# Seven products of half blocks in the second layer of an attention and feed-forward kernel

## The chip, the cores and the metric

The kernel runs on one core of a Trainium2 chip. A core has a matrix engine (PE, with its weight loads listed apart as PEld), a vector engine (DVE), a scalar engine (ACT), a general engine (POOL) and a queue engine (SP) that issues most DMAs. The metric is the device time of one execution in microseconds; of several runs the median is taken. Lower is better.

## The reference

Eight batches of 8 heads, 512 tokens, 32 states, head width 64. Tokens attend to states and states to tokens; the two results, 544 rows a batch, go through a two-layer network of width 512, 2048, 512 with a gate between the layers. All in float32.

```python
scores = scale * np.matmul(x, state.transpose(0, 1, 3, 2))
a = softmax(scores); xread = np.matmul(a, state)            # 512 token rows a batch
a2 = softmax(scale * np.matmul(state, x.transpose(...)))
sread = np.matmul(a2, x)                                    # 32 state rows a batch
x = np.concatenate([xread, sread], axis=2)...               # (8 * 544, 512)
h = x @ w_in
g = h * np.clip(h + 3.0, 0.0, 6.0) / 6.0
return g @ w_out
```

## The kernel before

**Joint weights.** `xread @ w_in` is `a @ (state @ w_in)`. So the kernel makes, for each batch, the joint weights `wp` (heads times states, 256 rows, by 2048 columns) and multiplies the attention weights `aT` by them; `xread` is never formed. The 2048 columns of the first layer lie in 16 blocks of 128. A **step** is one batch and one block: `first(n)` makes the first layer of the step in a PSUM bank `ps_h` (512 tokens wide), ACT and DVE make the gate `g` from it, `split` makes the pair `g_hi`, `g_lo`, and two steps later (`LAG = 2`) `second(n)` adds the block's share of the second layer to four banks `acc`, one for each 128 tokens. Steps 0 to 127 are the token rows of batches 0 to 7; steps 128 to 143 are the 256 state rows of all batches.

**Pairs.** A product of two float32 operands is made by `product` (line 1166) as three matmuls of 16-bit pairs, high by high, high by low, low by high (float32 rounded in batches 0 and 1, float16 from batch 2, `HALF_FROM = 2`). A step of the token rows has 6 matmuls in the first layer and 12 in the second, each 512 columns wide, each with a weight load of its own.

**Where the joint weights come from.** For batches 1 to 3 `wprime` makes them batch by batch on PE from float32 operands (line 631: 64 rows by 32 columns, eight tiles of the array side by side). For batches 4 to 7 `joined` (line 698) makes them for four batches at once, in eight calls between steps 33 and 72, from float16 pairs of `w_in` (`w_in_terms`); the results go out to DRAM, and `wprime_loaded` brings them back in each batch.

**The state rows.** Their first layer is made ahead of step 128 by `states_first`: seven products of half blocks (instead of eight) for each half of the columns, on sums of `w_in` that `w_in_terms` made and stored, with sums, gate, transposes and 32 small DMAs behind them. Steps 128 to 143 then only split and multiply by the second layer (`states_halves`).

**What sets the order.** `Plan.order` is a list scheduler: each operation has an engine (T is PE, V DVE, S ACT, P POOL, Q the SP queue), a cost, a rank (when it is due, in steps) and the keys it reads and writes; it places the ready operation of lowest rank and hands out buffers. Lists such as `PLANS`, `FETCH` and `CONVERTED` give ranks to the attention of the next batch and to conversions. Each engine then executes its list in order.

Of the kernel before, what the change touches and what calls it, by code (L numbers as in the profile page):

```python
# [46 lines left out]
CONVERTED = [23, 23, 21, 23, 25, 25, 30, 26, 36, 40, 38, 41, 35, 44, 43, 46]  # L47
EXTRA_FROM = 130
GROWN = {3: "ot", 4: "xb", 5: "raw", 6: "raw", 7: "ot"}
PLANS = [[0, 4, 10, 4, 5, 3, 12, 7], [-2, 5, -1, 16, 5, 4, 3, 7], [0, 1, 3, 8, 5, 3, 4, 8], [-3, -1, 6, 7, 5, 5, 6, 9], [-3, 3, 5, 4, 6, 2, 4, 7], [4, 6, -10, 11, 9, 10, -6, 11], [-2, 3, -2, 5, 4, 5, 15, 6]]  # L50
FETCH = [[4, 4], [19, 19], [25, 25], [43, 37], [57, 57], [64, 80], [93, 82]]
STATES_AT = 15
MAXIMA_AT = 22
WEIGHTS_AT = 17
OPENING_ROWS = 708
SQUEEZE = 0.5
PLAIN = 1
STATES = [108, 107, 116, 1.75, 1.5]
EARLY = 5
BY_TWO = (0, 0)  # L60
TERMS = [76, 4, 7.5]
JOINED = 4
JOINED_AT = [33, 38, 53, 57, 57, 64, 62, 72]
STATES_JOINED = 18
AHEAD = 5
FORCED = []
LOADED = [-5, 12.5]
STAGED = [('wp', 'wp'), ('ot', 'aT'), ('aT', 'ot'), ('ot', 'wp'), ('wp', 'wp'), ('aT', 'wp'), ('aT', 'wp'), ('wp', 'ot')]
PREP = [9, -27]
SUMS = 70  # L70
CURVE = 2
BY_SCALAR = ()

# [207 lines left out]
def tile_state_attention_then_hardswish_ffn(  # L281
# [65 lines left out]
            "raw": 3, "ot": 2, "xb": 1, "st_raw": 1, "stT": 2, "tmp": 8, "top": 2, "aT": 2, "m1": 3, "s1": 3, "nm2": 3, "r2": 2, "wp": 2, "g": 2,  # L347
# [41 lines left out]

    def get(key, make):  # L390

        if key[:2] not in made:
            made[key[:2]] = make()
        return made[key[:2]]
# [31 lines left out]

    plain = lambda b, i: b == 0 and i < PLAIN
# [197 lines left out]
    def all_heads(b, out, moving, by_pairs=False):  # L625

        for q in range(NQ):
            for u in range(NG):
                rows, cols = slice(u * D, (u + 1) * D), slice(q * NS, (q + 1) * NS)
                at = (q + 2 * u) % NQ if by_pairs else q  # L630
                nc.tensor.matmul(  # L631
                    out[q // 2 if by_pairs else u][at * NS : (at + 1) * NS, :],
                    made["stT", b][rows, cols], moving(q)[rows],
                    start=True, stop=True,
                )
# [14 lines left out]
    def states_joined(rank, after):  # L650

        n_b = B - JOINED
        raw_key, key = (("tmp", ("joined", k)) for k in ("raw", "all"))
        raw = lambda: tmp(raw_key).rearrange("p (b e) -> p b e", b=n_b)
        of_q = lambda t: t.rearrange("p (q n b) -> p b q n", q=NQ, b=n_b)
        for b in range(n_b):
            for u in range(NG):
                for k in range(D // NS):
                    rows = slice((u * D // NS + k) * NS, (u * D // NS + k + 1) * NS)
                    Q(rank, 25.0, lambda b=b, u=u, k=k, rows=rows: nc.sync.dma_start(  # L660
                        raw()[rows, b].rearrange("n (q c) -> n q c", c=NS),
                        st_v[JOINED + b, :, :, u, k * NS : (k + 1) * NS].rearrange("q n c -> n q c")),
                      (), [(*raw_key, b, u, k)], after, cost=0.65)
            V(0.22, rank, lambda b=b: nc.vector.transpose(
                of_q(tmp(key))[:, b], raw()[:, b].rearrange("p (q n) -> p q n", n=NS)),
                [(*raw_key, b, u, k) for u in range(NG) for k in range(D // NS)], [(*key, b)])
        plan.told += [None] * 6

    def states_paired(rank):
        key = ("tmp", ("joined", "all"))  # L670
        split(rank, lambda: states_16(0), lambda: states_16(1), lambda: tmp(key),
              [(*key, b) for b in range(B - JOINED)], [(*states_key, h) for h in range(2)], 0.62, "delta", X)

    states_key = ("tmp", ("joined", "16"))

    def states_16(h):
        return half_bits(tmp(states_key), 2 * S)[:, h * S : (h + 1) * S]

    def joined(p, m, s0):
# [40 lines left out]
        if s0 in FORCED:  # L720
            plan.ops[first_of[s0 - 2]][4].add(run_at)
# [750 lines left out]
    def w_in_terms(p, m, rank, after):  # L1472
# [17 lines left out]
        if m not in own:  # L1490
            after = [*after, *items]
# [348 lines left out]
```

## Time and profile before

| | |
|---|---|
| median of 3 runs | 616.17 us (614.4 to 618.34) |
| the profiled execution | 613.97 us, of it the span 612.2 us |
| PE busy | 605.7 us, 99% |
| DVE busy | 472.2 us, 77% |
| ACT busy | 334.8 us, 55% |
| POOL busy | 3.2 us, 1% |

PE's granted clock is at its upper level, 2.4 GHz, in every slice of the page after the first. A busy PE is one with a matmul in flight; the time from the start of one to the start of the next is what a matmul costs in a row of them, and it is shorter than the duration that is listed for one.

### The profile page before, as it was taken

Reading aid. Unit: us, or ns where it says so; the run is one execution under the profiler, and the core shown is the slowest. Engines: PE = TensorE matmul, PEld = TensorE weight load, DVE = VectorE, ACT = ScalarE, POOL = GpSimd, SP = SyncE. Lnnn points to the kernel's source line nnn. Section 1 sums busy time; section 2 is a strip of 40 time slices with the busy share of each in tenths; the row PEclk is TensorE's granted clock in tenths of the full one; section 3 lists DMA queues with packets and bytes.
Section 4 is the critical chain, followed back from the end, with each engine's and each line's share of the span. In section 5 each row is a group of like instructions: output and inputs, shape, how many; then the busy total and the mean of one; then the engine's idle time right before and its main releaser. Section 6 shows DMA issues by size and latency. Waiting matters only on the chain.

```text
span 612.2 us, 9806 instructions
## 1 busy us (share of the span) xinstructions
PE 605.7 (99%) x3650; PEld 320.7 (52%) x3650; DVE 472.2 (77%) x835; ACT 334.8 (55%) x560; POOL 3.2 (1%) x12
## 2 busy tenths in 40 slices
PE   9999999999999999999999999999999999999996
PEld 7677778777744444444444444444444444444443
DVE  6998999899989999886668746697879775355532
ACT  5888986346665556665465445444555454334332
POOL 2000000000000000000000000000000000000000
PEclk9999999999999999999999999999999999999999
DMA  8999122733673162327766262911740725551041
GB/s 290 371 235 272 52 70 35 126 113 54 96 194 54 37 172 101 146 84 176 176 232 198 53 154 54 224 38 31 178 172 15 220 87 180 187 177 31 7 131 34
DMA packets 154062, 80.45 MB, mean 131 GB/s; under 512 B 127648, under 2 KB 136224, under 8 KB 153888
## 3 DMA queue, kind: packets, MB, share of 16 engines
q1 hardware_dynamic: 153872, 79.77, 47.6%
q8 instruction: 28, 0.46, 0.3%
q14 instruction: 18, 0.15, 0.1%
q10 hardware_dynamic: 144, 0.07, 0.0%
HBM read 49.40 MB, written 24.64 MB: 121 GB/s over the span
## 4 chain that ended last, share of the span: by engine, by line
PE 90%; DMA 4%; DVE 4%; issue 1%; ACT 0%; SPq 0%; DVEq 0%
PE acc L1166 54%; PE ps_h L1166 25%; PE ps_s L1166 3%; DMA raw<-in_x_dram 2%; DMA early<-in_moe_w_out_dram 2%; PE ps_s L631 2%; PE ps_h L1123 1%; PE ps_s L698 1%; PE ps_h L698 1%; PE ps_h L631 1%; DVE w_in L502 1%; PE ps_h L1809 1%; PE acc L823 0%; DVE wp_lo L422 0%; DVE room L1354 0%
## 5 line engine op out<-in xcount | busy, mean ns | idle before, releaser
L1166 PE MATMUL acc<-w,g_hi 128*128 128x512 f16 x832 | 247.6, 379 | 0.0
L1166 PE MATMUL acc<-w,g_lo 128*128 128x512 f16 x416 | 157.7, 379 | 0.0
L1224 ACT ACTIVATE g<-ps_h,three,room 128x512 f32<-128x512 f32 x96 | 74.5, 776 | 112.7 <-PE ps_h L1166 108.2
L1227 DVE SCALAR_TENSOR_TENSOR g<-g,ps_h 128x512 f32<-128x512 f32 x128 | 87.0, 681 | 60.5 <-ACT g L1224 59.3
L1166 PEld LDWEIGHTS <-g_hi 128*128 128x128 f16 x832 | 80.0, 98 | 100.5 <-issue 6.1
L416 ACT ACTIVATE g_hi<-g 128x512 f16<-128x512 f32 x96 | 60.2, 628 | 56.3 <-DVE g L1227 45.9
L417 DVE SCALAR_TENSOR_TENSOR g_lo<-g,g_hi 128x512 f16<-128x512 f32 x96 | 65.9, 687 | 23.1 <-ACT g_hi L416 21.3
L1166 PE MATMUL ps_h<-aT_hi,wp_hi 128*128 128x512 f16 (+1 forms) x182 | 70.7, 389 | 0.5 <-DVE g L1227 0.5
L1166 PE MATMUL ps_h<-aT_lo,wp_hi 128*128 128x512 f16 (+1 forms) x182 | 69.6, 382 | 0.0
L1166 PE MATMUL ps_h<-aT_hi,wp_lo 128*128 128x512 f16 (+1 forms) x182 | 69.5, 382 | 0.0
L1166 PEld LDWEIGHTS <-g_lo 128*128 128x128 f16 x416 | 40.7, 98 | 49.1
L1166 PE MATMUL acc<-w_out_hi,g_hi 128*128 128x512 f32 x124 | 49.6, 400 | 0.0
L1166 PE MATMUL ps_h<-aT_hi,wp 128*128 128x512 f16 (+1 forms) x144 | 48.9, 380 | 0.0
L1166 PE MATMUL acc<-w_out_hi,g_lo 128*128 128x512 f32 x124 | 48.4, 390 | 0.0
L1166 PE MATMUL acc<-w_out_lo,g_hi 128*128 128x512 f32 x124 | 48.3, 389 | 0.0
L1166 PEld LDWEIGHTS <-wp_hi 128*128 128x128 f16 x256 | 25.1, 98 | 30.2
L1224 ACT ACTIVATE g<-ps_h,three 128x512 f32<-128x512 f32 x32 | 21.8, 686 | 17.2 <-PE ps_h L1166 15.8
L1166 PEld LDWEIGHTS <-wp 128*128 128x128 f16 x192 | 18.5, 98 | 22.8 <-issue 0.5
L1166 PEld LDWEIGHTS acc<-w_out_hi,g_hi 128*128 128x128 f32 x124 | 23.3, 188 | 9.3 <-issue 3.7
L1166 PE MATMUL ps_h<-aT_lo,wp 128*128 128x512 f16 (+1 forms) x72 | 27.4, 380 | 0.0
L1166 PEld LDWEIGHTS acc<-w_out_hi,g_lo 128*128 128x128 f32 x124 | 23.3, 188 | 5.0
L1166 PEld LDWEIGHTS acc<-w_out_lo,g_hi 128*128 128x128 f32 x124 | 23.3, 188 | 4.6
(222 smaller groups left out, 747.2 us busy)
## 6 DMA issues: line engine op xcount, KB each, us to landing
xb<-in_x_dram SPq DMA_DIRECT2D x32, 256.0 KB, 4.3
out_dram<-ot SPq DMA_DIRECT2D x8, 1024.0 KB, 4.8
raw<-in_x_dram SPq DMA_DIRECT2D x112, 64.0 KB, 2.7
far<-half SPq DMA_DIRECT2D x14, 512.0 KB, 3.4
terms<-far SPq DMA_DIRECT2D x14, 512.0 KB, 3.8
early<-in_moe_w_in_dram SPq DMA_DIRECT2D x5, 1023.0 KB, 6.9
raw<-raw SPq DMA_DIRECT2D x112, 32.0 KB, 2.0
raw<-in_moe_w_out_dram SPq DMA_DIRECT2D x7, 511.8 KB, 8.9
```

Source lines behind the costliest of these rows:

```text
L416: S(cost, rank, lambda: nc.scalar.mul(hi(), src(), by()), [*reads, *keys], [writes[0]], after)
L417: V_(cost, rank, lambda: nc.vector.scalar_tensor_tensor(lo(), src(), by(), hi() if hi().dtype == F16 else hi().bitcast(F32), op0=ALU.mult, ...
L502: nc.vector.scalar_tensor_tensor(d, low, 13, top_of(i).bitcast(U32), op0=ALU.logical_shift_right, op1=ALU.bitwise_or)
L631: nc.tensor.matmul(out[q // 2 if by_pairs else u][at * NS : (at + 1) * NS, :], made["stT", b][rows, cols], moving(q)[rows], start=True, st ...
L698: nc.tensor.matmul(bank(ps[i, u]), st(l)[rows, i], r()[rows, i], start=n == 0, stop=n == 2)
L1123: nc.tensor.matmul(bank(pr)[cols, u * D : (u + 1) * D], e2T(b, u)[:, j * P + q * NS : j * P + (q + 1) * NS], x_tile(b)[:, NG * q + u, j, : ...
L1166: nc.tensor.matmul(ps, l, r, start=start and k == 0, stop=stop and k == n - 1)
L1224: S_(cost + 0.05, rank, lambda: nc.scalar.activation(g(), bank(ps)[:, :width], AF.Relu, bias=three, scale=scales["1/h"]() if scaled else 1.0),
L1227: V(cost, rank, lambda: nc.vector.scalar_tensor_tensor(g(), g(), 6.0, bank(ps)[:, :width], op0=ALU.min, op1=ALU.mult), [ps], [g_key])
L1809: plan.issue(tc, lambda: nc.tensor.matmul(awake[:, :256], wake[:, :P], wake, start=True, stop=True), first_of["begun"])
```

## The change

Four edits, and ranks, buffers and lists changed with them.

- In batches 5 to 7 the second layer of the tokens is grouped: a step is now 256 tokens by two blocks (`first_grouped`, `second_grouped`), and its first layer is made of matmuls 256 columns wide. `SEVEN` names, by bits, the four groups of 256 tokens in which gates times output weights is made of seven products of half blocks instead of eight (batch 5 second group, batch 6 first, batch 7 both): the gate tile `G` holds 7 blocks of 128 columns, three of them sums made on DVE, `split` makes pairs 896 wide, the sums of the output weights `T7` are made once by `mixed_weights`, and at a group's end DVE joins the partial results.
- The input weights are converted once to float16 pairs that stay in SBUF (`w_in_paired`).
- The joint weights of batches 3 to 7 are made batch by batch on PE from float16 pairs (`wprime`, 24 matmuls for a chunk of 512 columns). `joined`, the stored joint weights and their DMAs are gone.
- The first layer of the state rows is made in steps 128 to 143 by plain products 256 columns wide (`first_states`). `states_first`, its sums, its transposes and its DMAs are gone.

```diff
 HALF_FROM = 2
+SEVEN = [0, 0, 0, 0, 0, 2, 1, 3]
+PAIRED = 3
+WPRIME_AT = [-3, -2, -2, -3]
+PAIRED_AT = [41, 32, 45, 46]
+MIXED_AT = [71, 45, 61, 59, 49, 56, 94, 78]
...
-JOINED = 4
-JOINED_AT = [33, 38, 53, 57, 57, 64, 62, 72]
...
     def wprime(b, parts, rank, banks=None, after=()):
...
         def run():
             for c, _, _, n, fs, bs in work:
+                if b >= PAIRED:
+                    for k, (l, r) in enumerate(((0, 0), (0, 1), (1, 0))):
+                        all_heads(b, [bank(k)[:, :n] for k in bs], lambda q: w_in_16(c, r)[:, q, fs], False, st_16[b](l), k)
+                    continue
                 all_heads(b, [bank(k)[:, :n] for k in bs], lambda q: w_in_of(c)[:, q, fs], b == 0)
...
+    def first_grouped(n):
+
+        b, i, _, _ = steps[n]
+        q, p = divmod(i, HF)
...
+            for k in range(2):
+                f = (2 * p + k) % FPC
+                fs = slice(f * P, (f + 1) * P)
+                product(bank(ps).rearrange("p (t k s) -> p t k s", k=2, s=P)[:, :, k],
+                        [((wh[:, u, fs], wl[:, u, fs]), (ah[:, u, ts], al[:, u, ts])) for u in range(NG)])
...
+        S_(0.73, rank, lambda: nc.scalar.activation(g(), h(), AF.Relu, bias=three, scale=scales["1/h"]()),
+           [ps, ("scale", "1/h")], [key])
+        V(0.63, rank, lambda: nc.vector.scalar_tensor_tensor(
+            g(), g(), 6.0, h(), op0=ALU.min, op1=ALU.mult), [ps], [key])
+        forms[n] = True
+        k0, k1 = 1, 5
+        if seven(b, q):
+            k0, k1 = 0, 7
+            for cost, out, one, other, op in (
+                (0.4, (5, 7), (3, 5), (1, 3), ALU.subtract), (0.53, (0, 7, 3), (3, 6), (4, 7), ALU.add),
+            ):
...
+        split(ahead(n), lambda: operand_of(n, "hi", width), lambda: operand_of(n, "lo", width), src_, [key],
+              [("g_hi", n), ("g_lo", n)], 0.08 + 0.00105 * width, G_SCALE / 4)
...
+    def second_grouped(n):
...
+        for j, parts in (
+            (0, ((0, 2, lambda: half(w(1), 0)), (1, 6, lambda: half(w(1), 1)))),
+            (2, ((0, 1, lambda: half(w(0), 0)), (1, 3, lambda: t(0)))),
+            (3, ((0, 0, lambda: t(1)), (1, 5, lambda: t(3)))),
+            (1, ((0, 4, lambda: t(2)),)),
+        ):
+            def run(j=j, parts=parts):
+                for k, a, right in parts:
+                    product(bank(acc(j))[:, k * W : (k + 1) * W], [(a_of(a, 7 * P), right())],
+                            opens and k == 0, closes and k == parts[-1][0])
+            T(0.328 * len(parts), rank, run, keys, [acc(j)])
...
+    def mixed_weights(p, rank, after):
...
-    def states_first(p, rank, after=()):
...
+    def first_states(n):
...
+            product(bank(ps)[:, :width], [((w_in_16(c, 0)[:, q, fs], w_in_16(c, 1)[:, q, fs]), (ah[:, q], al[:, q]))
+                                          for q in range(NQ)])
...
-        if 0 < b < JOINED and n % (2 * FPC) == 0:
+        if 0 < b < B and not grouped(b) and n % (2 * FPC) == 0:
             wprime(b, [(c, 0, FPC), (c + 1, 0, FPC)], n - 2.6, None, [first_of[n - 3]])
             plan.ops[first_of[n - 2]][4].add(wp_at[b, c, 0])
-        elif JOINED <= b < B and n % FPC == 0:
-            wprime_loaded(b, c, n + LOADED[1], [first_of[n + LOADED[0]]])
+        elif grouped(b) and (i in (0, FPC) if BY_PAIRS else i < HF and i % 2 == 0):
+            c, many = i // 2, 2 if BY_PAIRS else 1
+            s = n + WPRIME_AT[c]
+            wprime(b, [(c + k, 0, FPC) for k in range(many)], s - 2.6, None, [first_of[s - 3]])
+            plan.ops[first_of[s - 2]][4].add(wp_at[b, c, 0])
```

**PE in batch 7.** Of the program before, the end of one product of the state rows' first layer (`terms`), the start of a first layer of the tokens, and the start of a second layer:

```order
L1166 MATMUL ps_s<-terms,aT_lo 128x512
L1166 LDWEIGHTS wp
L1166 MATMUL ps_h<-aT_hi,wp 128x512
L1166 LDWEIGHTS wp
L1166 MATMUL ps_h<-aT_lo,wp 128x512
...
L1166 LDWEIGHTS g_hi
L1166 MATMUL acc_5470<-w_1479,g_hi 128x512
L1166 LDWEIGHTS g_hi
L1166 MATMUL acc_5470<-w_1479,g_hi 128x512
L1166 LDWEIGHTS g_lo
L1166 MATMUL acc_5470<-w_1479,g_lo 128x512
```

Of the changed program, the end of the second layer of a step with seven products (`T` is `T7`) and the start of the next step's:

```order
L1125 MATMUL acc_6021<-T_2771,g_lo 128x256
L1125 LDWEIGHTS g_hi
L1125 MATMUL acc_6029<-T_2771,g_hi 128x256
L1125 LDWEIGHTS g_hi
L1125 MATMUL acc_6029<-T_2771,g_hi 128x256
L1125 LDWEIGHTS g_lo
L1125 MATMUL acc_6029<-T_2771,g_lo 128x256
L1125 LDWEIGHTS g_hi
L1125 MATMUL acc_6004<-w_1480,g_hi 128x256
```

A seven-product step has 12 matmuls in its first layer and 21 in its second, all 256 wide, where a step before has 6 and 12 of 512; every one keeps its own weight load, and the state rows' products no longer stand between the steps. Counted over the program, 1440 matmuls are 256 wide now (576 first layers of the tokens, 672 seven products, 192 first layers of the state rows); of those 512 wide, 384 fewer are in the tokens' second layer, 288 fewer in their first, and the 84 of `states_first` are gone.

**DVE in batch 7.** Of the program before, the gates (`g`, L1227) and second halves (`g_lo`) of two steps, among the state rows' work (L1570, L1545):

```order
L1227 SCALAR_TENSOR_TENSOR g_5759<-g_5759,ps_h_5745 128x512
L417 SCALAR_TENSOR_TENSOR g_lo_5783<-g_5759,g_hi_5770 128x512
L1227 SCALAR_TENSOR_TENSOR g_5792<-g_5792,ps_h_5776 128x512
L417 SCALAR_TENSOR_TENSOR g_lo_5800<-w_in2_5692,g_hi_5794 128x256
L1570 TENSOR_TENSOR C_5633<-ps_s_5785,C_5633 128x512
L1545 SCALAR_TENSOR_TENSOR raw_5809<-raw_5809,C_5633 128x1024
L417 SCALAR_TENSOR_TENSOR g_lo_5829<-g_5792,g_hi_5821 128x512
```

Of the changed program, two steps with seven products:

```order
L1180 SCALAR_TENSOR_TENSOR G_4142<-G_4142,ps_h_5969 128x512
L1189 TENSOR_TENSOR G_4142<-G_4142 128x256
L1189 TENSOR_TENSOR G_4142<-G_4142 128x3x128
L1180 SCALAR_TENSOR_TENSOR G_4142<-G_4142,ps_h_5988 128x512
...
L415 SCALAR_TENSOR_TENSOR g_lo_6059<-G_4142,g_hi_6040 128x896
L415 SCALAR_TENSOR_TENSOR g_lo_6076<-G_4142,g_hi_6061 128x896
```

Where a step before has two DVE operations 512 wide (gate and `g_lo`), this one has four: the gate, two with sums of blocks (256 and 384 wide), and `g_lo` 896 wide. Two steps go through together: both gates with their sums, then both `g_lo`.

## Rows read from the trace of the kernel before

**Rows 1.** The page's head: span, and busy time by engine.

```profile
span 612.2 us, 9806 instructions
PE 605.7 (99%) x3650; PEld 320.7 (52%) x3650; DVE 472.2 (77%) x835; ACT 334.8 (55%) x560; POOL 3.2 (1%) x12
```

**Rows 2.** Waits of PE: engine, line, releaser: us in total, times, longest.

```profile
PE ps_h L1809 <- PEq L1824: 0.8, 1, 0.8
PE ps_h L1166 <- DVE g L1227: 0.5, 1, 0.5
```

**Rows 3.** Chain of waits, two neighbouring pieces of one step: start us, us, what.

```profile
360.74 2.59 PE acc L1166 x12
363.33 1.29 PE ps_h L1166 x6
```

**Rows 4.** Groups of PE by form: line, operands, shapes, count | busy us, mean ns.

```profile
L1166 PEld LDWEIGHTS <-g_hi 128*128 128x128 f16 x832 | 80.0, 98 | 100.5 <-issue 6.1
...
L1166 PE MATMUL ps_s<-terms,sums 128*128 128x512 f16 x48 | 11.7, 379 | 0.0
...
L1166 PE MATMUL ps_s<-terms,aT_hi 128*128 128x512 f16 x24 | 7.1, 379 | 0.0
...
L1166 PE MATMUL ps_s<-terms,aT_lo 128*128 128x512 f16 x12 | 4.5, 379 | 0.0
```

**Rows 5.** Timeline of the opening: start us, us from first to last, instruction, count.

```profile
8.17 0.60 PE L823 MATMUL acc<-ident,xb 128*128 128x128 f32 x4
8.61 0.89 PE L898 MATMUL acc<-sread_t,w_in 128*128 128x64 f32 x7
...
12.78 0.88 PEld L1809 LDWEIGHTS <-const-bfloat16-1.0 128*128 128x128 bf16 x8
...
12.89 1.06 PE L1809 MATMUL ps_h<-const-bfloat16-1.0 128*128 128x256 bf16 x8
```

**Rows 6.** Timeline of PE around one call of the joined weights.

```profile
209.58 0.38 PE L1166 MATMUL acc<-w,g_lo 128*128 128x512 f16 x1
209.89 0.82 PE L698 MATMUL ps_s<-half,tmp 64*128 64x512 f16 x6
210.55 0.81 PE L698 MATMUL ps_h<-half,tmp 64*128 64x512 f16 x6
211.29 0.61 PE L1166 MATMUL acc<-w,g_hi 128*128 128x512 f16 x2
```

**Rows 7.** Timeline of PE around float32 joint weights of batch 3, two chunks.

```profile
257.20 0.38 PE L1166 MATMUL acc<-w,g_lo 128*128 128x512 f16 x1
257.51 1.09 PE L631 MATMUL ps_s<-w_in,stT 64*32 64x512 f32 x16
...
259.39 0.61 PE L1166 MATMUL acc<-w,g_hi 128*128 128x512 f16 x2
```

**Rows 8.** Busy time by stretch: PE, PEld, DVE, ACT, POOL, then clock, DMA.

```profile
50.00:100.00 50.00, 49.53 (x336) 37.25 (x334) 48.19 (x85) 42.13 (x87) 0.00 (x0) 1.00 0.33 97
...
400.00:450.00 50.00, 50.00 (x274) 22.57 (x276) 40.25 (x63) 24.71 (x38) 0.00 (x0) 1.00 0.41 107
...
500.00:550.00 50.00, 50.00 (x234) 22.67 (x232) 25.80 (x37) 19.95 (x29) 0.00 (x0) 1.00 0.54 179
```

**Rows 9.** Groups of DVE by form.

```profile
L1227 DVE SCALAR_TENSOR_TENSOR g<-g,ps_h 128x512 f32<-128x512 f32 x128 | 87.0, 681 | 60.5 <-ACT g L1224 59.3
L417 DVE SCALAR_TENSOR_TENSOR g_lo<-g,g_hi 128x512 f16<-128x512 f32 x96 | 65.9, 687 | 23.1 <-ACT g_hi L416 21.3
...
L417 DVE SCALAR_TENSOR_TENSOR half<-raw,room,half 128x1024 f16<-128x1024 f32 x8 | 10.2, 1278 | 1.2 <-ACT half L416 1.2
...
L417 DVE SCALAR_TENSOR_TENSOR g_lo<-w_in,g_hi 128x256 f16<-128x256 f32 x16 | 6.8, 424 | 12.6 <-ACT g_hi L416 12.6
```

**Rows 10.** Groups of ACT by form.

```profile
L1224 ACT ACTIVATE g<-ps_h,three,room 128x512 f32<-128x512 f32 x96 | 74.5, 776 | 112.7 <-PE ps_h L1166 108.2 <-DVE room L1404 1.7 <-DVE raw L1089 1.2
L416 ACT ACTIVATE g_hi<-g 128x512 f16<-128x512 f32 x96 | 60.2, 628 | 56.3 <-DVE g L1227 45.9 <-PE acc L1166 10.3
```

More of the change, by code (lines that the diff above doesn't have):

```diff
@@ L388, in raw_tile, with quarter @@
         return stage.tile(list(shape), dtype, name="raw", **by_plan("raw", key)) if t is None else t
+    def quarter(key, shape, dtype=F16):
+        pool = gp if key[0] == "wp" else att
+        return get(("place", key), lambda: pool.tile(list(shape), dtype, name=key[0], **by_plan(key[0], key)))
     def get(key, make):
@@ L632, in all_heads @@
                     out[q // 2 if by_pairs else u][at * NS : (at + 1) * NS, :],
-                    made["stT", b][rows, cols], moving(q)[rows],
-                    start=True, stop=True,
+                    (made["stT", b] if left is None else left)[rows, cols], moving(q)[rows],
+                    start=not term, stop=term in (None, 2),
                 )
@@ L648, in all_heads_apart @@
                     )
[L650 to L667, printed above, removed]
@@ new lines, in pair_key, with w_in_16, pair_reads, wp_key @@
+    def pair_key(c):
+        return (f"w_in{c - 1}", "pair") if c else ("w_in", "pair")
+    def w_in_16(c, h):
+        shape = (P, 2, NQ, CH)
+        return get(pair_key(c), lambda: region(NCH - 1, shape, F16, "pair") if c == 0 else cpool.tile(
+            list(shape), F16, name="pair", tag=f"w_in{c - 1}"))[:, h]
+    def pair_reads(c, ks=range(2)):
+        return [(*pair_key(c), k, h) for k in ks for h in range(2)]
+    def wp_key(b, c, h):
+        if b >= HALF_FROM:
+            return ("wp", (b, c))
+        return ("ot", ("wp", b, c)) if 0 < b and (NCH * b + c) % 3 == 2 else ("wp", (b, c, h))
@@ L1169, in tile_state_attention_then_hardswish_ffn, with ahead, seven, G_of @@
     first_of = {}
+    def ahead(n):
+        return n if n < URGED[0] else 0.02 * n + URGED[1]
+    def seven(b, q):
+        return SEVEN[b] >> q & 1
+    def G_of(n):
+        key = ("G", n)
+        return get(key, lambda: grown_half(key))
+    def grown_half(key):
+        place = plan.home[key[:2]]
+        if place not in G_tiles:
+            if "w_in" not in G_tiles:
+                G_tiles["w_in"] = cpool.tile([P, 2, 2 * J, P], F32, name="G", tag=f"w_in{NCH - 1}")
+            G_tiles[place] = G_tiles["w_in"][:, place]
+        return G_tiles[place]
@@ L1171, in first @@
     def first(n):
         b, i, _, _ = steps[n]
+        if grouped(b):
+            first_grouped(n)
+            return
         ps = ("ps_h", n)
@@ L1229, in first @@
         if not in_32:
-            split(n, half["hi"], half["lo"], g, [g_key], [("g_hi", n), ("g_lo", n)], cost,
+            split(ahead(n), half["hi"], half["lo"], g, [g_key], [("g_hi", n), ("g_lo", n)], cost,
                   G_SCALE if scaled else None)
@@ L1431, in w_16_of, with region_gone @@
         return w_16[c][:, k % FPC]
+    def region_gone(n):
+        c, half = REGIONS[n]
+        fs = range(c * FPC, (c + 1) * FPC)
+        assert all(f in in_16 for f in fs)
+        return [m for f in fs for m in plan.readers[w_out_key(f, half)]]
     region_free = {}
@@ L1456, in converted @@
         at_16[k] = [hi16, lo16]
-        for n, (c, half) in enumerate(REGIONS):
-            if n >= NCH - 1 and n not in grown and all(f in in_16 for f in range(c * FPC, (c + 1) * FPC)):
-                grown.add(n)
-                if GROWN.get(n):
-                    plan.grow(GROWN[n], [m for f in range(c * FPC, (c + 1) * FPC) for m in plan.readers[w_out_key(f, half)]], n)
-    at_16, grown = {}, set()
-    in_16 = set()
-    pieces, operands, items, joined_of = [], [], [], {}
-    OPERANDS = (1, 2, 5, 6, 3, 4, 7)
@@ L1628, in tile_state_attention_then_hardswish_ffn @@
+    chunks, steps, segment_of = [], [], []
+    for b in range(B + 1):
+        for i in range(NF):
+            if i % FPC == 0:
+                chunks.append((b, i // FPC))
+            n = HF if grouped(b) else NF
+            steps.append((b, i, i % n == 0, i % n == n - 1))
+            segment_of.append((b, i // n))
     first_after = {}
```

456 lines of the change are left out of this document (176 added, 280 removed), and 24 rows, old and new, of the table OPENING.

## The prediction

> **What bounds the kernel now.** First the page's head: PE is busy in 605.7 of 612.2 us, DVE in 77%, ACT in 55% [rows 1]. A busy share alone would not settle it, so second the waits: after the opening the longest list entry of PE is 0.5 us, once [rows 2]. Third the chain of waits: its long middle is PE following PE, pieces of 12 matmuls in 2.59 us and 6 in 1.29 [rows 3], so 0.216 us from start to start for one float16 matmul of 512 columns, and the step of 18 costs 3.88. Nothing else is seen between the pieces. The kernel is a queue of matmuls, and a change is worth what it does to the sum of their spacings, as long as DVE keeps up. How near DVE is to its end is the fourth view: from 50 to 100 us it is busy 48.2 of 50, and PE still 49.5; from 400 to 450 it is 40.3, from 500 to 550 25.8 [rows 8]. So this order of work bears a DVE at 96%.
>
> **The change, part by part, on PE.**
>
> Removed:
> - Matmuls of 512 columns: 384 in the second layer (the grouped steps with seven products no longer have them), 288 in the first layer of batches 5 to 7, 84 in the state rows' seven products (48 + 24 + 12 [rows 4]). 756 x 0.216 = 163.2 us [rows 3].
> - `joined`: eight calls. One call runs from the end of the last slot before it (209.58 + 0.216 = 209.80) to 211.29, 1.49 us [rows 6]; eight are 12.0 us. Six slots of pairs side by side would be 1.30, so 0.20 of it goes into turning the array from one tiling to another and back.
> - The float32 joint weights of batch 3: two calls of 257.20 + 0.216 to 259.39 = 1.97 us [rows 7], 3.9 us.
>
> Together 179.1 us.
>
> Added:
> - 1440 matmuls 256 columns wide. Half of a 512 would be 0.108, but each still has its own weight load of 0.098 us [rows 4], so the load nearly fills the slot, and half is only the lower bound. The nearest row is in the opening: 8 matmuls of 16 bits, 256 wide, each with its load; the loads run 0.88 us, seven spacings and one load, so (0.88 - 0.10) / 7 = 0.111 [rows 5]. The other is the transposes, which stream as long: four from 8.17 to 8.61, 0.110 [rows 5]. I take 0.110, between the bound and the nearest row and close to that; rounding leaves that row open to 0.112, the upper bound. 1440 x 0.110 = 158.4 us (155.5 to 161.3).
> - The joint weights of batches 3 to 7 on PE from float16 pairs. No row shows float16 in eight tiles; `joined` is the nearest (float16, pairs of tiles, load hidden) and the float32 call shows that the eight tiles run side by side. A chunk is 24 matmuls, eight at a time, three slots of 0.216, and the turn of 0.20: 0.85 us. Twelve calls have one chunk (batches 5 to 7), 10.2 us; four have two (batches 3 and 4), 1.49 each as `joined`, 6.0 us. Together 16.2 us. Were the load of 0.098 not hidden in any slot, it would be 20 chunks x 3 x 0.098 = 5.9 us more, the upper bound; at the lower, the turns of the sixteen calls cost nothing, 3.2 us less.
>
> Together 174.6 us. **PE's sum: 174.6 - 179.1 = -4.5 us**, with the bounds of the 256-wide price alone -7.4 to -1.6.
>
> The Trainium skill (TensorE: Matmul & The Clock Gate, section Back-to-back issue gap) gives N / 2.4 + 2.5 ns for a warm matmul, 109.2 ns at 256 columns; by that, as an estimate, the sum would be -5.7 us. The opening's row at 0.111 says a little more than the page, and no row here says it for float16 weights that differ.
>
> **On DVE.** A seven-product step has the gate (0.68), sums 256 and 384 wide (0.42 and, between 0.42 and 0.69, 0.56), and `g_lo` 896 wide, between 0.69 and 1.28: 1.13 [rows 9]. That is 2.79 us against 1.37 for a step before, and its PE time is 33 x 0.110 = 3.63. Added too are 32 short operations for the mixed weights with their splits (about 4.3 us for each of eight, steps 45 to 94), eight `pair` conversions at 1.28 in place of sixteen `half` ones, and the joins at the end of four groups. Gone are the state rows' sums, gates and transposes, the `w_in` sums and the joined halves; the halves of the joint weights stay 8 a batch. So the early stretch, now at 96%, gets no fuller, and the late one (80 and 52%) fills up. A batch has about 17 us of the next batch's attention on DVE (22 operations of about 0.69 [rows 9] and some 2 us of small ones) and 5.5 of halves. Batch 6: 8 x 2.79 + 8 x 1.37 + 17 + 5.5 = 56 us, against PE's 8 x 3.63 + 8 x 3.91 + 3.4 for joint weights + 2 for scores = 66. That is 85%, under what the trace bears. ACT stays well under it. So I cost DVE at nothing but new waits of 0.5 us; what hides it is the next batch's attention being spread over a whole batch. If that clumps, rival 2 applies.
>
> **On SP, DMA and the ends.** About 140 DMAs go away and nothing waited for them; no gain. The opening's first 30 steps have the same work in the same order. In the last 16 steps PE now makes first layers, 2.6 us a step, and the chain behind one (ACT, DVE, ACT, DVE, each about 0.42 [rows 9]) has two steps of room; only at the last one can it show, inside the 0.5.
>
> **Sum:** -4.5 + 0.5 = -4.0 us. Against the profiled execution, 613.97, that is 610.0; the median of the runs shown stands 2.2 us above it, so 616.17 - 4.0 = **612.2 us**.
>
> **The rivals.**
> 1. *The 256-wide matmuls cost what half a 512 does and the tiled calls hide their turns in part.* 1440 x 0.108, joint weights 1 us cheaper, no new wait: -8.4 us, 607.8. For it: at 512 columns the load is wholly hidden. Against: the row at 0.111. Chance 0.20.
> 2. *DVE becomes late in the seven-product groups.* A gate there has ACT 0.78, DVE 0.68 + 0.98, ACT about 1.0 (0.63 at 512 columns, 896 here), DVE 1.13 behind it [rows 9, 10], 4.6 us with no handoffs, of 7.3 in two steps; other DVE work that comes in between has 1.7 us of room for a pair of steps. If half of a batch's attention falls into the seven-product half, DVE there has 8 x 2.79 + 8.7 + 2.8 = 33.8 us against PE's 32: 2 us lost in each of three such halves, and as much again in handoffs, +4 to +8 on the sum of PE: about 617. For it: the order puts two gates together ahead of two `g_lo`. Against: 96% was borne. Chance 0.17.
> 3. *Slower: the weight load does not fit behind 256 columns.* The place is all 1440 matmuls. A load starts with the matmul before it and lasts 0.098 us; the slot is 0.108. The sum turns at (179.1 - 16.2) / 1440 = 0.113, just above the opening's row, and 1% is lost from 0.117. With 0.120, loads that start 0.01 late, it is +10 us: 626. For it: the opening's row already lies above half of a 512, and its operands are a constant. Against: transposes with 32-bit loads keep 0.110. Chance 0.10. The Trainium skill (same page and section) says that a stream of loads and matmuls runs at 81 ns for 128 columns where an isolated one takes 56, that is, that loads show once matmuls are short; the opening's row agrees in direction, with 3 ns instead of 25.
>
> The forecast has the other 0.53.
>
> **Range and chances.** A measurement of this kernel tells about 1%, 6 us, from no change. The low end is PE's best sum without waits, -7.4, and 2 us for the scatter of the medians: 607. The high end takes in rival 2 and the unhidden loads of the joint weights: 620. Rival 3 is left out. Faster by over 1% (below 610): rival 1 and the lower part of the forecast, 0.20 + 0.12 = 0.32. Slower by over 1%: rival 3 and the end of rival 2, 0.13. Within 1%: 0.55.
>
> **What would show it.** The spacing of 256-wide matmuls in a seven-product step: 0.110 (0.108 rival 1, 0.117 and more rival 3). A single-chunk call of the joint weights: 0.85 us from slot to slot. PE's waits for `g_hi` and `g_lo` in batches 5 to 7: under 1 us in all (rival 2: 4 or more), DVE there at 85 to 90%. No `joined` pieces and no products between steps 108 and 128. I am wrong if PE's waits add up to more than the 4 us that its sum gives back, or if the 256-wide spacing depends on the operand.

## The result and the profile after

The changed kernel takes **610.0 us** (median; 608.65 to 610.17) against 615.69 for the kernel before in the same comparison: ratio 0.9897, 95% interval 0.9861 to 0.9934. Timed again beside other kernels it took 609.71, ratio 0.9905 (0.9889 to 0.992). That is 5.7 to 6.1 us, 1.0%, and the interval excludes no change. The forecast was 612.2 us in 607 to 620. The kernel before has one run more here than in the table ahead of the prediction, so its median is 615.69 and not 616.17.

The head of the page after, to be read against [rows 1]:

```profile
span 608.4 us, 11646 instructions
PE 600.8 (99%) x4654; PEld 387.0 (64%) x4654; DVE 505.8 (83%) x925; ACT 352.5 (58%) x587; POOL 3.3 (1%) x12
```

PE issues 1004 matmuls more in less time, and the work that pays for it is on DVE: 505.8 us instead of 472.2. PE's waits after (engine, line, releaser: us in total, times, longest), against [rows 2]:

```profile
PE ps_h L1772 <- PEq L1787: 0.8, 1, 0.8
PE acc L779 <- DMA xb<-in_x_dram: 0.4, 1, 0.4
PE ps_h L1125 <- DVE wp L420: 0.4, 1, 0.4
PE ps_s L631 <- DVE w_in L502: 0.4, 1, 0.4
PE ps_h L1125 <- DVE g L1349: 0.3, 1, 0.3
```

All are of the opening or of the early float32 batches; none names the tiles of a grouped step (`G`, `g_hi` or `g_lo` from `G`, `ot`). The chain of waits in batch 5, against [rows 3]:

```profile
443.40 2.29 PE acc L1125 x21
445.69 1.31 PE ps_h L1125 x12
```

2.29 / 21 and 1.31 / 12 are both 0.109 us for a matmul of 256 columns, PE still following PE. Over all such pairs of neighbours in the trace the mean from start to start is 0.1092 us. The timeline of PE's loads and of PE for one first layer of such a step:

```profile
513.90 1.30 PEld L1125 LDWEIGHTS <-wp 128*128 128x128 f16 x12
...
514.01 1.47 PE L1125 MATMUL ps_h<-aT,wp 128*128 128x256 f16 x12
```

Twelve loads span 1.30 us, eleven spacings and one load of 0.10: 0.109 again. One call of the new joint weights, on PE's timeline, which answers to [rows 6, 7]:

```profile
499.22 0.38 PE L1125 MATMUL ps_h<-aT,wp 128*128 128x256 f16 x2
499.53 0.84 PE L631 MATMUL ps_s<-pair,st 64*32 64x512 f16 x24
500.31 0.60 PE L1125 MATMUL acc<-w,g_hi 128*128 128x512 f16 x2
```

The slot of the last 256-wide matmul ends at 499.22 + 2 x 0.109 = 499.44, so the call takes 0.87 us to 500.31. The twelve calls of one chunk all take 0.87 us, the four of two chunks 1.51. DVE by form (count, then busy us and mean ns of one), against [rows 9]:

```profile
L415 DVE SCALAR_TENSOR_TENSOR g_lo<-G,g_hi 128x896 f16<-128x896 f32 x32 | 34.7, 1086 | 4.1 <-ACT g_hi L414 3.6
...
L1180 DVE SCALAR_TENSOR_TENSOR G<-G,ps_h 128x512 f32<-128x512 f32 x48 | 32.8, 683 | 14.0 <-ACT G L1178 13.9
...
L1189 DVE TENSOR_TENSOR G<-G 128x384 f32<-128x384 f32 x32 | 17.9, 558 | 1.1
L1189 DVE TENSOR_TENSOR G<-G 128x256 f32<-128x256 f32 x32 | 13.6, 425 | 1.1
```

And busy time by stretch (stretch, its length, then PE, PEld, DVE, ACT, POOL, granted clock, DMA share, GB/s), against [rows 8]: the early stretch, and those of a group of seven in batches 5, 6 and 7.

```profile
50.00:100.00 50.00, 49.64 (x336) 37.36 (x335) 48.67 (x86) 42.17 (x86) 0.00 (x0) 1.00 0.36 108
...
420.00:451.00 31.00, 31.00 (x395) 25.11 (x393) 27.27 (x46) 17.59 (x26) 0.00 (x0) 1.00 0.23 53
451.00:482.00 31.00, 31.00 (x273) 24.32 (x271) 28.14 (x47) 18.68 (x30) 0.00 (x0) 1.00 0.09 15
514.00:545.00 31.00, 31.00 (x286) 27.79 (x285) 25.94 (x50) 17.35 (x22) 0.00 (x0) 1.00 0.00 1
```

DVE is at 88, 91 and 84% there, and PE is busy throughout.

### The profile page after: what moved, and what is told of

It is laid out like the page before. It is cut to its first block, busy times and chain, and to the rows that moved or that the text cites. A ratio compares the mean times of both kernels' runs of the same rounds, so it can differ in the third digit from the quotient of the medians.

```text
span 608.4 us, 11646 instructions
## 1 busy us (share of the span) xinstructions
PE 600.8 (99%) x4654; PEld 387.0 (64%) x4654; DVE 505.8 (83%) x925; ACT 352.5 (58%) x587; POOL 3.3 (1%) x12
## 4 chain that ended last, share of the span: by engine, by line
PE 89%; DMA 6%; DVE 2%; SPq 0%; issue 0%; ACT 0%; DVEq 0%; ACTq 0%
PE acc L1125 54%; PE ps_h L1125 29%; PE ps_s L631 4%; DMA early<-in_moe_w_in_dram 3%; DMA raw<-in_x_dram 2%; PE ps_h L1082 1%; PE ps_h L631 1%; DMA xb<-in_x_dram 1%; DVE w_in L502 1%; SPq L597 0%; DVE g_lo L420 0%; DVE aT L420 0%; DVE wp L420 0%; PE ps_s L1082 0%; SPq L617 0%
## 5 line engine op out<-in xcount | busy, mean ns | idle before, releaser
L1125 PE MATMUL acc<-w,g_hi 128*128 128x512 f16 (+1 forms) x768 | 204.7, 353 | 0.0
L1125 PE MATMUL ps_h<-aT,wp 128*128 128x256 f16 (+2 forms) x1050 | 188.1, 324 | 0.7 <-DVE wp L420 0.4
L1125 PE MATMUL acc<-w,g_lo 128*128 128x512 f16 (+1 forms) x384 | 135.3, 352 | 0.0
L1125 PEld LDWEIGHTS <-wp 128*128 128x128 f16 x864 | 84.2, 98 | 44.4 <-issue 0.8
L1178 ACT ACTIVATE G<-ps_h,three,room 128x512 f32<-128x512 f32 x48 | 37.4, 778 | 49.9 <-PE ps_h L1125 48.3
L414 ACT ACTIVATE g_hi<-G 128x896 f16<-128x896 f32 (+2 forms) x64 | 46.8, 734 | 32.9 <-DVE G L1189 19.8
L1346 ACT ACTIVATE g<-ps_h,three,room 128x512 f32<-128x512 f32 x48 | 37.2, 776 | 47.9 <-PE ps_h L1125 47.8
L415 DVE SCALAR_TENSOR_TENSOR g_lo<-G,g_hi 128x896 f16<-128x896 f32 (+2 forms) x64 | 52.2, 819 | 12.4 <-ACT g_hi L414 11.7
L1125 PE MATMUL acc<-T,g_hi 128*128 128x256 f16 x256 | 43.7, 273 | 0.0
L1125 PE MATMUL acc<-T,g_lo 128*128 128x256 f16 x128 | 34.9, 273 | 0.0
```

The source lines that it names most:

```text
L414: S(cost, rank, lambda: nc.scalar.mul(hi(), src(), by()), [*reads, *keys], [writes[0]], after)
L415: V_(cost, rank, lambda: nc.vector.scalar_tensor_tensor(lo(), src(), by(), hi() if hi().dtype == F16 else hi().bitcast(F32), op0=ALU.mult, ...
L1125: nc.tensor.matmul(ps, l, r, start=start and k == 0, stop=stop and k == n - 1)
L1178: S_(0.73, rank, lambda: nc.scalar.activation(g(), h(), AF.Relu, bias=three, scale=scales["1/h"]()), [ps, ("scale", "1/h")], [key])
L1346: S_(cost + 0.05, rank, lambda: nc.scalar.activation(g(), bank(ps)[:, :width], AF.Relu, bias=three, scale=scales["1/h"]() if scaled else 1.0),
```

## The experiments

Two questions stood after the result: which part of the change brings the 6 us, and which of the rivals was near. All kernels are edits of the changed one. The chip's times of the kernel before were 615.1 to 615.9 us beside them.

**The change again, as the yardstick.**

> The changed kernel once more, beside the next three on the same chip, as their reference. 0.990 of the kernel before (610 us).

609.71 us, as above; its span is 607.4 against 608.4 in the first profile. The difference of 1 us between two executions of one kernel lies in the opening, where PE's waits after the first entry are 0.2 us each instead of 0.3 to 0.4.

**No group of seven; nothing grouped.**

```diff
-SEVEN = [0, 0, 0, 0, 0, 2, 1, 3]
+SEVEN = [0, 0, 0, 0, 0, 0, 0, 0]
```

> SEVEN is all zero, so no batch is grouped: batches 5 to 7 run steps of 512 columns as before, no gate sums, no mixed weights; the input pairs, the per-batch joint weights and the plain first layer of the state rows stay. Theory (sum of PE's spacings, 0.109 us for 256 columns and 0.216 for 512): back come 384 + 288 matmuls of 512 (145.2 us), away go 1248 of 256 (136.0), and six calls of two joint chunks (8.9) stand for twelve of one (10.2): +7.9 us on the changed kernel, about 618, that is 2 us above the kernel before: the rest of the change pays nothing by itself. Rival (the gain comes from the rest, fewer DMAs and no joined call, and the seven products only pay their own way): within 2 us of the changed kernel, 608 to 612.

616.13 us, ratio to before 1.0007 (0.9989 to 1.0026). So by the medians the rest of the change (input weights as pairs, joint weights by batch, state rows by plain products) gives nothing and costs nothing, and the groups of seven bring 6.4 us. The expectation was 1.5 us higher; the traces place this difference below, behind the next kernel.

**Grouped steps, but eight products in all of them.** Here the grouping stays (256 columns in the first layer, two blocks a step) and only the saved eighth goes.

```diff
-    grouped = lambda b: b < B and SEVEN[b] > 0
+    grouped = lambda b: 5 <= b < B
```
with `SEVEN` all 0.

> Batches 5 to 7 stay grouped (steps of 256 tokens by two blocks, first layer 256 wide), but all six groups use eight products, no sums, no mixed weights. Theory (PE's sum): in 32 steps 12 matmuls of 512 (2.59) stand for 21 of 256 (2.29): +9.7 us on the changed kernel, about 619.7, with DVE emptier. Rival (DVE's sums, joins and mixed weights hold PE up somewhere in the changed kernel, so that seven products give less than PE's sum): +4 to +7, 614 to 617.

618.33 us, ratio 1.0044 (1.0031 to 1.0058): 8.6 us above the change, where the theory said 9.7 and the rival 4 to 7. Grouping alone costs some 2 us, the seven products give 8.6 back.

Both kernels came out under the sum of PE's spacings, by 1.5 and 1.1 us. The traces show where: take the start of one matmul that all of them have, the 361st of 512 columns into `acc`, in the second layer of batch 1, and the time from there to the end of the span (us, one profiled execution each).

| kernel | this matmul starts | from there to the end |
|---|---|---|
| before | 161.4 | 450.7 |
| the change | 163.0 | 445.4 |
| the change again | 162.0 | 445.4 |
| no group | 160.8 | 452.9 |
| grouped, eight products | 161.7 | 454.9 |

Behind this point the change gains 5.3 us, and without groups it is 7.4 us longer, with eight products 9.5. With the measured prices (0.1092 for 256 columns, 0.216 for 512, 0.87 and 1.51 for a call) the sums are 7.5 and 9.6. So behind the opening the sum on PE holds to 0.1 us; there the groups of seven bring 7.4 us and the rest of the change costs 2.1. What is missing from the medians does not lie there; the opening alone differs by 1.0 us between the two executions of the change.

**Is a short matmul held up by its weight load?** This is the mechanism of rival 3, driven further: each 256-column matmul of the grouped first layers is cut into two of 128 columns.

```diff
-                product(bank(ps).rearrange("p (t k s) -> p t k s", k=2, s=P)[:, :, k],
-                        [((wh[:, u, fs], wl[:, u, fs]), (ah[:, u, ts], al[:, u, ts])) for u in range(NG)])
+                for t in range(2):
+                    tt = slice(q * W + t * P, q * W + (t + 1) * P)
+                    product(bank(ps).rearrange("p (t k s) -> p t k s", k=2, s=P)[:, t, k],
+                            [((wh[:, u, fs], wl[:, u, fs]), (ah[:, u, tt], al[:, u, tt])) for u in range(NG)])
```

> In the 48 grouped steps of batches 5 to 7 each matmul of 256 columns into ps_h (576 of them) is cut into two of 128 columns, each with its own weight load; nothing else changes. My theory (a load is hidden behind the columns that stream, so the engine pays its columns and a few ns for each instruction): 1152 at about 0.056 us against 576 at the 0.109 us of the changed kernel, +1.7 us, about 611.5 us. The theory of the third rival (a load of 128 columns shows where the stream is shorter than the load's own row, 98 ns): 1152 at 0.098, +50 us, about 660 us. The Trainium skill's sustained figure for 128 columns (TensorE: Matmul & The Clock Gate, 81 ns) would give 1152 at 0.081, +30.5 us, about 640 us. Any value between says by how much the load outlasts 128 columns.

611.2 us (610.23 to 612.4): +1.5 on the yardstick, where my theory said +1.7 and the others +30 and +50. Its timelines of PE and of PE's loads for one first layer:

```profile
513.77 1.50 PE L1125 MATMUL ps_h<-aT,wp 128*128 128x128 f16 x24
515.11 0.38 PE L1125 MATMUL acc<-w,g_hi 128*128 128x256 f16 x2
```

```profile
513.66 1.44 PEld L1125 LDWEIGHTS <-wp 128*128 128x128 f16 x24
```

24 matmuls take (515.11 - 513.77) / 24 = 0.056 us each. A load is listed with 0.10 us, yet 24 of them go out in 1.44 us, 23 spacings and one load, so one each 0.058: as listed, neighbouring loads overlap, so the duration of one load says nothing on how often one can start. Rival 3 is dead at 256 columns, and at 128.

**A fifth group of seven.** If DVE has room, one more group is 2.4 us by PE's sum.

```diff
-SEVEN = [0, 0, 0, 0, 0, 2, 1, 3]
+SEVEN = [0, 0, 0, 0, 0, 2, 3, 3]
```

> SEVEN = 0,0,0,0,0,2,3,3: the second group of batch 6 uses seven products too, five groups instead of four. PE's sum alone: 8 steps x 0.303 = -2.4 us on the changed kernel, about 607.6. Rival (DVE is the bound there): batch 6 then has on DVE 16 x 2.75 + 17 of attention + 5.5 of joint halves + 2.4 of joins = 69 us against PE's 63, so PE waits 3 to 8 us in batch 6 and the kernel is 1 to 6 us slower than the changed one, 611 to 616, with DVE at 95% or more there.

630.75 us, ratio 1.0249: 21 us slower than the change, and neither case had foreseen it. PE's longest waits in it:

```profile
PE acc L1125 <- ACT ot L1217: 6.1, 1, 6.1
PE ps_h L1125 <- ACT aT L414: 4.8, 2, 4.1
PE ps_h L1125 <- DVE G L1180: 3.4, 4, 2.5
```

and two of its stretches:

```profile
482.00:514.00 32.00, 25.33 (x298) 18.71 (x298) 23.96 (x43) 12.39 (x19) 0.00 (x0) 0.84 0.15 34
545.00:575.00 30.00, 20.94 (x155) 16.65 (x154) 19.68 (x40) 11.64 (x15) 0.00 (x0) 0.77 0.10 36
```

DVE is at 75 and 66% in the stretches with the stops, which looked like order, not load: in DVE's list the last batch's attention (`aT`) stood behind two transposes and four joins, and joins, ranked behind every gate, kept an `ot` buffer, so that the eviction waited for a transfer out and PE for its accumulators. Theory A was that: order. Theory B was that DVE has no room for a fifth group, and that its low share is seen only after PE has stopped and sends it less work. Three kernels change only the order of the five groups.

```diff
-            V(cost, n + LAG + 1, lambda o=o, one=one, other=other, op=op: nc.vector.tensor_tensor(
+            V(cost, ahead(n), lambda o=o, one=one, other=other, op=op: nc.vector.tensor_tensor(
```

> The kernel with five groups of seven (630.8 us), with one edit: the four joins of a group's blocks in ot (L1255) get the rank of a gate instead of one step later, so that they no longer stand behind every gate in VectorE's order. If the loss of the five groups is order and latency (a late join keeps an ot buffer, the eviction waits for the transfer out, TensorE for its accumulators: 6.1 us in that profile, plus the lower granted clock behind it), this wait goes and the late aT stays: about 620 to 625 us. If the loss is VectorE's sum of work, which is not changed, it stays at 630 within 2.

620.92 us, ratio 1.0078: the wait for `ot` is gone, as theory A said, and the one for `aT` is now 7.4 us.

```diff
-PLANS = [..., [-5, 1, 5, 11, 7, 3, 14, 7]]
+PLANS = [..., [-5, 1, 5, 5, 7, 3, 7, 9]]
```

> The kernel with five groups of seven (630.8 us), with one edit: the ranks of the last batch's attention are moved up (PLANS of batch 7: 11 to 5 for the sums of the softmax, 14 to 7 for the states' sums, 7 to 9 for the moved weights), so that aT is made ahead of the two transposes and the four joins that stood before it. If order is the cause, TensorE's wait for aT (4.8 us) goes and the one for the ot buffer stays: about 620 to 626 us. If VectorE's sum is the cause: 630 within 2.

620.5 us, ratio 1.0067. Each edit alone returns 10 us, but here not by the waits that theory A had named: the one for `aT` falls from 4.8 to 1.6 us, the one for `ot`, which was to stay, is gone too, and gates are late in its place:

```profile
PE ps_h L1125 <- DVE G L1180: 7.2, 4, 3.5
```

> The kernel with five groups of seven (630.8 us), with both edits: joins ranked as gates, and the last batch's attention moved up. If order and latency are the whole loss, both waits go and the time comes to the sum on TensorE, 64 matmuls of 512 columns fewer at 0.216 us against the changed kernel's groups, so 607.6 us, or up to 612 with the short waits left. If VectorE's sum of work is the limit, 625 to 631 us, since that sum is not changed.

618.88 us, ratio 1.0047 (1.0031 to 1.0063): not 607.6 to 612, and below theory B's 625 as well. Two returns of 10 us make 12 together: each edit alone had already removed the wait for `ot`. One long wait is left, and the stretches show what stands around it, the last of them the stop itself:

```profile
PE ps_h L1125 <- ACT aT L414: 6.0, 1, 6.0
```

```profile
482.00:514.00 32.00, 24.03 (x250) 17.98 (x248) 27.41 (x47) 15.37 (x24) 0.00 (x0) 0.89 0.09 25
...
500.00:510.00 10.00, 3.92 (x38) 1.97 (x38) 8.00 (x16) 3.13 (x7) 0.00 (x0) 0.66 0.16 57
...
499.50:505.70 6.20, 0.26 (x3) 0.09 (x1) 5.93 (x12) 2.23 (x5) 0.00 (x0) 0.73 0.23 86
```

PE loses 8 of 32 us, and DVE, which it waits for, is at 86% all the same. While PE stands, from 499.5 to 505.7, DVE works 5.93 of 6.20 us: it has a queue of softmax, joins and transposes to get through. Its idle time comes behind the stop, when PE has sent it nothing, as theory B said. The next kernel moves the same attention so early that nothing of it can be late.

```diff
+PLANS = [..., [-5, 1, 3, 3, 3, 3, 5, 11]]
```

> As the kernel with both edits (618.9 us; TensorE still waits 6.0 us for aT of the last batch, which VectorE makes last, at some 500 us), with the last batch's whole softmax some 30 VectorE instructions earlier (its ranks 5, 5, 7, 7 become 3, 3, 3, 5), ahead of a fused weight that it stood behind. If the order on VectorE is the whole cause, the wait for aT goes and the time is 608 to 612 us. If VectorE has no room between 451 and 514 us (busy 28.1 of 31 and 27.4 of 32 us there), the wait only changes its name, to gates (G) or g_lo, and the time stays at 615 to 620 us.

618.71 us, ratio 1.0038 (1.0018 to 1.0058). The wait for `aT` is gone and others have its place, some 20 us earlier:

```profile
PE ps_s L631 <- ACT tmp L984: 4.8, 2, 4.6
PE acc L1125 <- DVE g_lo L415: 2.8, 3, 1.4
```

The time is what theory B said. The names are so in part: the longer wait is for `tmp`, the exponentials of the states' softmax on ACT, but ACT waits there for row maxima from DVE, and DVE again works through the stop:

```profile
479.80:484.40 4.60, 0.05 (x1) 0.06 (x1) 4.40 (x9) 2.03 (x5) 0.00 (x0) 0.95 0.00 0
```

Theory A is not borne out for the 9 us that none of the three orders returned. Then the fifth group in another place:

```diff
-SEVEN = [0, 0, 0, 0, 0, 2, 1, 3]
+SEVEN = [0, 0, 0, 0, 0, 3, 1, 3]
-MIXED_AT = [71, 45, 61, 59, 49, 56, 94, 78]
+MIXED_AT = [71, 45, 61, 59, 49, 56, 73, 76]
```
with the joins ranked as gates.

> Five groups of seven as before, but the fifth is the first group of batch 5 in place of the second of batch 6 (SEVEN 3, 1, 3 for batches 5 to 7), with two of the mixed weights made earlier and the joins ranked as gates. By the sum on TensorE 607.6 us. If VectorE's room in the stretch is what counts: the 32 us of a group of seven take some 11 us more of VectorE, and around batch 5 the changed kernel has it busy 21.6 of 25, 14.8 of 20 and 27.3 of 31 us, so there is more room than beside the last batch's attention (28.1 of 31, 24.9 of 32): 607 to 611 us. If any fifth group is too much: 615 us or more, with waits for G, g_lo or aT around 380 to 450 us.

620.44 us, ratio 1.0072, as the last of the three cases said. I had seen more room in batch 5 than there is; its stretches:

```profile
380.00:400.00 20.00, 19.49 (x178) 17.07 (x177) 19.26 (x31) 9.63 (x13) 0.00 (x0) 1.00 0.56 126
400.00:420.00 20.00, 18.27 (x200) 14.83 (x197) 18.52 (x33) 12.43 (x20) 0.00 (x0) 1.00 0.11 33
420.00:451.00 31.00, 23.69 (x250) 16.59 (x238) 24.56 (x43) 13.89 (x22) 0.00 (x0) 0.89 0.16 35
```

DVE at 96 and 93% for 40 us, and PE stops behind it (4.8 us of waits for `aT`, 2.8 for `g_lo`). It remained to take work off DVE. First by giving joins and mixed weights to the idle POOL:

```diff
-            V(cost, ahead(n), lambda ...: nc.vector.tensor_tensor(
+            P_(2 * cost, ahead(n), lambda ...: nc.gpsimd.tensor_tensor(
```
and the same for the sums in `mixed_weights`.

> The kernel of five groups with both edits (618.9 us), and 68 operations taken from VectorE to the idle GpSimd: the four joins of each of the five groups (20, some 2.5 us a group) and the 48 sums of the mixed weights (some 2.9 us for each of eight). One 128x512 operation takes GpSimd 1.27 us in the opening where VectorE takes 0.69. If VectorE's room is what stops the fifth group (busy 27.4 of 31, 28.1 of 31, 27.4 of 32 us between 420 and 514, TensorE's wait 6.0 us with the clock at 0.66 of full for 10 us behind it), some 5 us less work there shrinks or removes the wait: 608 to 614 us. If it is only the latency of one chain, or if GpSimd slows VectorE by as much as it takes over, 617 us or more.

630.18 us, ratio 1.0229: 11 us worse than before the move. POOL's timeline has the four joins of one group, DVE's timeline shows what ran beside them:

```profile
456.78 5.69 POOL L1255 TENSOR_TENSOR ot<-ot 128x512 f32<-128x512 f32 x4 [186.10 <-DVE G L1189]
```

```profile
455.76 1.02 DVE L1189 TENSOR_TENSOR G<-G 128x256 f32<-128x256 f32 x2
...
456.96 0.68 DVE L980 TENSOR_REDUCE nm<-ps_s 128x1 f32<-128x512 f32 x1
...
458.35 2.12 DVE L415 SCALAR_TENSOR_TENSOR g_lo<-G,g_hi 128x896 f16<-128x896 f32 x1
460.39 0.67 DVE L1180 SCALAR_TENSOR_TENSOR G<-G,ps_h 128x512 f32<-128x512 f32 x1
461.10 1.78 DVE L1189 TENSOR_TENSOR G<-G 128x256 f32<-128x256 f32 x2
```

While POOL adds (456.78 to 462.47), a `g_lo` takes 2.12 us instead of 1.09 and a pair of sums 1.78 instead of 1.02; the two operations that read PSUM keep their 0.68. The Trainium skill (SBUF — State Buffer, section Who interferes with whom) says that a DVE instruction with two SBUF inputs contends with a GpSimd instruction that reads SBUF; these rows agree. The 68 operations had taken DVE 36.7 us in the kernel with both edits; moving them lightens DVE by only 11.8 (519.1 to 507.3), so most of the work came back as longer instructions.

The 11 us themselves are not lost beside the last batch's attention. They stand earlier, between 250 and 320 us; the sums of the mixed weights run on POOL until 271:

```profile
250.00:290.00 40.00, 36.84 (x247) 16.41 (x252) 27.50 (x37) 18.24 (x27) 16.66 (x17) 1.00 0.22 36
290.00:320.00 30.00, 23.34 (x254) 10.03 (x239) 20.25 (x39) 13.11 (x23) 0.00 (x0) 0.83 0.47 101
...
482.00:514.00 32.00, 30.96 (x328) 25.10 (x326) 30.14 (x46) 18.64 (x27) 5.32 (x4) 1.00 0.05 18
```

PE loses 10 us between 250 and 320, in waits for `wp` (3.2 us) and `aT` (6.1), with a granted clock of 0.83 as the mean from 290, where it lost nothing before the move; what made this `aT` late was not followed. Between 420 and 545 it is busy 120.2 us instead of 116.1, and the wait of 6.0 us is gone. So the joins on POOL do relieve the late stretch, as theory B would have it, and the sums of the mixed weights on POOL, with the order that came with them, cost more than that. The last kernel takes the joins away and gives them to nobody.

```diff
-        for cost, o, one, other, op, reads, writes in (
...
-        store()
+        store(4)
```

> The kernel of five groups with both edits (618.9 us), without the joins: the 20 operations of VectorE that add up the seven evicted blocks of a group are left out, and the last four blocks are stored as they are (the output of these groups is left incomplete). That takes 2.5 us a group from VectorE, 5 us of it between 451 and 520 us, and gives nothing to another engine. The order around the last batch's attention stays nearly the same (aT some eight instructions earlier in VectorE's list). If VectorE's room is what stops the fifth group: the wait of 6.0 us for aT shrinks by about those 5 us, with the lower clock behind it, 608 to 613 us. If another chain is the cause: 616 us or more.

**610.08 us** (609.3 to 611.12), 8.8 less than with the joins, for 20 operations of 0.43 to 0.69 us. The late batches' waits for DVE are down to this:

```profile
PE acc L1125 <- DVE g_lo L415: 1.2, 2, 0.8
```

The stretches of 420 to 451, 451 to 482, 482 to 514 and 514 to 545 us together, in the change, with both order edits, with the attention earlier still, and without joins:

```profile
sum 125.00, PE 125.00 PEld 97.65 DVE 106.28 ACT 70.00 POOL 0.00; mean PE 31.25 PEld 24.41 DVE 26.57 ACT 17.50 POOL 0.00
```

```profile
sum 125.00, PE 116.10 PEld 96.95 DVE 109.78 ACT 67.73 POOL 0.00; mean PE 29.02 PEld 24.24 DVE 27.45 ACT 16.93 POOL 0.00
```

```profile
sum 125.00, PE 117.07 PEld 97.69 DVE 110.22 ACT 67.50 POOL 0.00; mean PE 29.27 PEld 24.42 DVE 27.56 ACT 16.88 POOL 0.00
```

```profile
sum 125.00, PE 123.26 PEld 104.70 DVE 111.07 ACT 72.98 POOL 0.00; mean PE 30.81 PEld 26.18 DVE 27.77 ACT 18.24 POOL 0.00
```

In these three kernels with five groups DVE does 110 or 111 us of work in the 125, and PE gets 116, 117 or 123 us out of that, by how much work each of its steps asks of DVE. The 88 to 89% is no limit of the engine: shorter stretches above have 91% (the change) and 96% (the fifth group in batch 5). It is the share that is left when DVE is full at the stops and idle behind them. Read in the same way, DVE is busy 93 to 99% of the longest stops of all five kernels that change the order or the place (6.23 of 6.70 us with the joins first, 7.12 of 7.20 in three stops with the attention first, 3.52 of 3.80 in batch 5). The long wait for `ot` in the first kernel with five groups was another thing: DVE works 2.26 of its 6.00 us, and each of the orders removed it, so theory A explains that part. Taking 12 us of work from DVE over the whole run (519.1 to 507.4), 2.5 us a group, removed a stop that three changes of order had only moved about; that `aT` also comes eight instructions earlier does not explain it, since thirty instructions earlier had returned nothing; and the joins of the four other groups had no wait to give back, as the change has none there. So DVE's work around the last batch's attention, and not its order alone, keeps a fifth group from paying. The run does not reach the 607.6 of PE's sum: 2.5 us stay lost, PE is still idle for 1.7 us between 482 and 514, and without the joins the scheduler orders that stretch a little otherwise. No kernel with five groups that computes the whole result beat the change; at 610.0 us it stays the fastest.

## Why the prediction was right

- **What bounds it.** A queue of matmuls, worth the sum of their spacings: borne out. PE's sum was to move 4.5 us and, with 0.5 of new waits, the time 4.0. The medians moved 5.7 to 6.1. Behind the opening the traces moved 5.3, and the same sum with the measured prices is 5.5.
- **256 columns at 0.110.** Measured 0.1092, in both layers and three batches; 1440 x 0.0008 = 1.2 us of the difference is this term. The row I leaned on, 0.111 in the opening, has the same form but a constant operand. The Trainium skill's estimate (TensorE: Matmul & The Clock Gate, section Back-to-back issue gap) of 109.2 ns and -5.7 us was the nearest of all; the section calls it the gap of an isolated matmul, and here it is that of a stream. The same section's 81 ns for 128 columns with their loads is not what this chip did: 56 ns.
- **Joint weights 16.2 us.** The calls measured 0.87 and 1.51 instead of 0.85 and 1.49, so 16.5. The turn from one tiling to another and back, taken over from `joined`, was the right term.
- **New waits 0.5 us.** None in the grouped steps; the opening's waits vary by 1 us from run to run instead, as the two profiles of the change show. So the forecast's +0.5 was not needed. With the 1.2 above, less the 0.3 of the joint weights, it makes 1.4 us of the miss of about 2; the rest is no more than the opening's scatter.
- **DVE at 85%, borne.** The price of a step was right (1.086 for 1.13, 0.558 for 0.56). The mean over 125 us is 85%; the share is 88 and 91% in two of the stretches with a group of seven, and PE never waited for it.
- **Rival 1** (0.108 and hidden turns, 607.8): the spacing lies between its 0.108 and the forecast's 0.110, nearer to the forecast; on the turns it was wrong. **Rival 2** (DVE late) had the right mechanism one group too soon: at four groups it costs nothing, at five 9 to 21 us, more than its price of 4 to 8. I had left out what a stop of PE does to the clock behind it, 1.5 us in the kernel with both order edits; the waits themselves, 9.0 us between 420 and 545, were longer than priced too. **Rival 3** fell with the 128-column run; my argument for it, that a load of 0.098 nearly fills a slot of 0.108, read a duration as if it were a spacing.

Where the time came from: the groups of seven, 6.4 us by the medians and 7.4 behind the opening, against the ungrouped kernel. The other three edits, which the sum had as removals of 34 us and additions of 37, cost 2.1 us behind the opening; the medians do not show it.

## What to carry to other kernels

Price a stream of matmuls by the time from start to start, never by the listed duration of a matmul or of a load. When an edit moves work from the bounding engine to the next one, look at that engine stretch by stretch, and at the very time of a stop: here 85% over 125 us cost nothing, and one group more cost 9 to 21 us in every order tried, with a mean of 88% that hid 5.93 of 6.20 us at the stop, though 97% was borne from 50 to 100 us, in another mix of instructions. Engine time that seems free on POOL is not all free: of 36.7 us taken from DVE, 11.8 stayed gained, since DVE's own operations on SBUF became longer beside POOL's. Compare spans from a point behind the scatter: here a common matmul at 161 us made differences of 0.1 us readable where the medians gave 1.

## What the runs showed of the hardware

- A float16 load of 128 x 128 is listed with 98 ns, yet pairs of load and 128-column matmul follow each other in 56 ns.
- A POOL addition of 128x512 in SBUF takes 1.44 us (15 of them) against 0.69 on DVE, and DVE instructions with two SBUF inputs run up to twice as long beside it.
- A stop of PE is dearer than its wait. In the kernel with both order edits, behind the wait of 6.0 us, matmuls of 256 columns follow each other in 0.22 us instead of 0.109, at a granted clock of 0.50 (1.2 GHz) from 506 to 508 us. The twelve matmuls of this first layer take 2.8 us without their second wait of 0.35, where 1.3 is usual:

```profile
505.72 0.37 PE L1125 MATMUL ps_h<-aT,wp 128*128 128x256 f16 x1 [5.96 <-ACT aT L414]
506.45 2.50 PE L1125 MATMUL ps_h<-aT,wp 128*128 128x256 f16 x11 [0.35 <-DVE aT L415]
```
